# Output phase of an adaLN / S4 / SwiGLU kernel: the layout of the convolution's z rows for six token tiles, and the place of the block sums of x

## The chip, the cores and the metric

The kernel runs on one NeuronCore of a Trainium2 chip. The metric is the device time of one execution in microseconds (us). The engines are named as the profile names them: PE (matmul), PEld (weight load), DVE (vector), ACT (scalar), POOL and SP (which here only issues DMAs). ACT and POOL issue DMAs too; the profile calls the issuing side SPq, ACTq and POOLq.

## The reference

```python
x = A_u                                            # 1 x 2048 x 640, float32
mod = (_silu(c) @ w_mod).reshape(c.shape[0], 6, 1, -1)
sa, ca, ga, sb, cb, gb = (mod[:, 0], mod[:, 1], mod[:, 2], mod[:, 3], mod[:, 4], mod[:, 5])
h = _layernorm(x, axis=-1) * (1 + ca) + sa
x = x + ga * _A_ref(h, ...)                        # S4: K = sum_n C exp(dt A l) dt B, y = causal conv(h, K) + h * D
h = _layernorm(x, axis=-1) * (1 + cb) + sb
x = x + gb * _B_ref(h, w1, w3, w2)                 # (silu(h @ w1) * (h @ w3)) @ w2, inner width 1728
```

The long convolution is done through a two-stage transform by matmuls. The second stage of the inverse transform, per token tile, is what the change touches: y = i2 times z, added to x.

## The kernel before, in words

**Stages.** Up to about 366 us the kernel makes the S4 kernel K, transforms, multiplies and stores the half-inverted result `z` to DRAM (`zs`). Then come layernorm and the MLP on 16 token tiles of 128 tokens by 640 channels. The MLP works in two pairs of 1024 tokens: pair 0 is tiles 0 to 7, pair 1 tiles 8 to 15; within a pair, "A" is the first four tiles and "B" the last four. The inner width 1728 is cut into 14 blocks f of 128 (the last of 64).

**Products.** Operands are split into a high and a low part (`xA0` holds both, `gh` and `gl` a weight's), and each product takes three matmuls: high by high, high by low, low by high. In pair 0 the blocks f = 0, 13, 1, 2 (`simple`) are computed plainly (`plain`): first for A in this order, then for B in the order 2, 1, 13, 0. The other ten go through `seven`, which makes the four quarter products of a block out of seven by sums of x and of the weights. The sums of x are `x_sums` (DVE subtractions on the raw tiles s0 to s8) and `x_sum_split` (an ACT cast and a DVE subtraction for each of T10, T20, T40 and T11, T21, T41). The split of the B operands themselves is in `x_turn` and `x_split`: four transposes, ACT's affine step into a room s, ACT's cast to the high part, DVE's subtraction for the low part. The last of the five is T31 (k = 1). In `plain` the B operands are used in the order k = 4, 0, 2, 3, 1, that is xB4, T30, xB2, xB3, T31.

**Output phase.** `outputs` multiplies h with w2 in 28 steps (14 for A, 14 for B). A step has a w2 load issued on ACT's queue for four steps ahead (`load(n + 4, S)`), the operands of the next step (`operands(n + 1)`: ACT casts gh and uh, DVE makes gl and ul), the side work `side(n)`, and then 15 matmuls. Inside it `in_order[0]` is set, so each engine keeps the order of the program; the helper that records this is line 114, which is why the profile shows nearly every instruction at L114.

**Side work.** In pair 0's output phase `prepare` makes tiles 8 to 15 ready for pair 1. Per tile: `x_get` issues the loads on SP (x, and z from `zs`), `x_mid` multiplies z by `i2` into two PSUM banks, adds to x, and takes the layernorm's statistics, `x_norm` normalizes on ACT, and `turn_a` or `turn_b` transposes. The steps are fixed by tables:

```python
mids = (3, 4, 5, 6, 8, 9, 10, 12)
norms = (5, 6, 7, 8, 11, 12, 13, 15)
gets = (0, 0, 1, 2, 3, 4, 4, 6)
homes = (("xA0", "xA1"), ("xA2", "xA3"), ("xA4", "xB2"), ("xB3", "xB4"), ("T40", "T20"), ("T10", "T30"),
         None, None)
```

`homes` gives the first six of these tiles two rooms each to hold z, which are operand rooms of pair 0 that are no longer read; the last two use a `z_tile` of their own (name A).

**z in a tile.** A tile's z has 64 rows (two of them, real and imaginary, for each of 32), 4 token blocks b and 5 channel blocks k of 128. Channel blocks 0 and 1 go to partitions 0 to 63 and blocks 2, 3 and 4 to partitions 64 to 127, so that two row groups of PE work side by side. `z_load` issues one DMA per channel block. In `x_mid` each (token block, row group) pair is one matmul with 64 rows and 32 output columns: eight in all, on eight different parts of the array, 256 wide for the lower rows and 384 wide for the upper (`ZW`).

**DMA counters.** The framework gives each DMA of the hardware queues one of eight completion counters, DMAHW0 to DMAHW7, in turn as they stand in the program; SP and ACT share them. Before it is issued, a DMA waits until the last DMA on its counter has landed. In the built program T40's first transfer waits on DMAHW6, and the w2 loads for later steps on the counters of xA, xB and T transfers.

Of the kernel before, what the change touches and what calls it, by code (L numbers as in the profile page):

```python
# [9 lines left out]
F32 = mybir.dt.float32  # L10
# [12 lines left out]
DC = 128  # L23
NDC = D // DC
# [95 lines left out]
def tile_kernel(ctx: ExitStack, tc: tile.TileContext, a):  # L120
    nc = tc.nc
    V, S, G, PE = nc.vector, nc.scalar, nc.gpsimd, nc.tensor
# [8 lines left out]
    i2 = cp.tile([P, NA], F32, name="i2")  # L131
# [10 lines left out]
    V, S, G, PE, Q = (InOrder(tc, e, (front,)) for e in (nc.vector, nc.scalar, nc.gpsimd, nc.tensor, nc.sync))  # L142
# [633 lines left out]
    def zj(k, j):  # L776
        return zs[k, j % 4, j // 4].rearrange("l c f d -> (c f) l d")
# [66 lines left out]
        moments.extend((mv, rs))  # L844
        return power

    def z_load(z, j, ks, q=nc.sync, b0=0):

        nb = z.shape[1]
        for k in ks:  # L850
            hh = int(k > 1)
            kk = k - 2 * hh
            ins = q.dma_start(z[hh * 64:hh * 64 + 64, :, kk * DC:kk * DC + DC], zj(k, j)[:, b0:b0 + nb])
        return ins

    def x_tile():
# [5 lines left out]
    def z_tile():  # L862
        z = tz.tile([P, SD, 3, NA], F32, name="A")
        return z.rearrange("p k s b -> p (k s b)").rearrange("p (b d) -> p b d", b=4)

    ZW = (2 * DC, 3 * DC)
# [136 lines left out]
    for word in FRONT:  # L1003
        name, k = word[:2].rstrip("+"), int(word[len(word[:2].rstrip("+")):])
# [25 lines left out]
    for rnd in range(NS // EB):  # L1030
        if 2 <= rnd < 7:
            late_load(rnd - 2)
        for word in ROUND:
            name, k = word[:2].rstrip("+-"), EB * rnd + int(word[len(word[:2].rstrip("+-")):])
# [16 lines left out]
    for tk in range(NS + 1, LAG + 8 * NDC + 2):  # L1051
# [17 lines left out]
        i = tk - 1 - LAG - 8 * NDC + 8  # L1069
# [37 lines left out]
    V, S, G, PE = (InOrder(tc, e, (in_order,)) for e in (nc.vector, nc.scalar, nc.gpsimd, nc.tensor))  # L1107
    SQ = InOrder(tc, nc.sync, (in_order, sp_order))
# [3 lines left out]
    def bank(g):  # L1112
        return psG.tile([P, 512], F32, name="ps", tag="g") if g else psA.tile([P, 512], F32, name="ps", tag="acc")
# [13 lines left out]
    def pair_tile(name, dt=F32R):  # L1127

        return wq.tile([P, 2, 512], dt, name=name)
# [20 lines left out]
    def x_get(j, x, loaded=False, homes=None):  # L1150

        if homes:
            zs_ = [pair_tile(n, F32).rearrange("p a b -> p (a b)")[:, :768].rearrange("p (b d) -> p b d", b=2)
                   for n in homes]
        else:
            zs_ = [z_tile()]
        with tc.issue_after(zlast[0].ins):
            if not loaded:
                SQ.dma_start(x, a["x"][j * P:(j + 1) * P, :])
            for i, z in enumerate(zs_):  # L1160
                z_load(z, j, range(NDC), SQ, 2 * i)
        return [x, [zs_[b * len(zs_) // 4][:, b % (4 // len(zs_))] for b in range(4)]]

    def x_mid(j, got, g):

        x, z = got
        py = [bank(g) for _ in range(2)]
        for b in range(4):
            for hh in range(2):
                r, c = slice(hh * 64, hh * 64 + 64), slice(b * NA, b * NA + NA)  # L1170
                n = ZW[hh]
                PE.matmul(py[hh][c, :n], i2[r], z[b][r, :n], start=True, stop=True, tile_position=(r.start, c.start))
        for hh in range(2):
            h = slice(hh * 256, hh * 256 + ZW[hh])
            V.tensor_tensor(x[:, h], py[hh][:, :ZW[hh]], x[:, h], op=OP.add)
        got.extend(ln_stats(xp, x))
        G.dma_start(xs[j], x)
# [8 lines left out]
    ends = [None, None]  # L1186

    def x_split(name, xf):
        t = pair_tile(name)
        ends[0] = S.copy(t[:, 0], xf)  # L1190
        ends[1] = V.tensor_tensor(t[:, 1], xf, t[:, 0].bitcast(F32), op=OP.subtract)
        return t[:, 0], t[:, 1]
# [26 lines left out]
    def x_sums(i, which=range(4)):  # L1219

        if 0 in which:
            xraw["s", i] = xraw["A", i], xraw["A", i + 2], xraw["B", i], xraw["B", i + 2]
        b11, b21, b12, b22 = xraw["s", i]
        for n in which:
            to, l, r = ((b11, b12, b11), (b12, b22, b12), (b22, b22, b11), (b21, b21, b22))[n]
            V.tensor_tensor(to, l, r, op=OP.subtract)
        xraw["T1", i], xraw["T2", i], xraw["T4", i] = b11, b22, b21

    def x_sum_split(i, names=("T1", "T2", "T4")):
        for n in names:  # L1230
            xop[n, i] = x_split(f"{n}{i}", xraw[n, i])
# [44 lines left out]
    def plain_weights(f, after=None):  # L1276
        g = split(weight(f, "wg"), WS, ("gh", "gl"), after)
        return g, split(weight(f, "wu"), WS, ("uh", "ul"), after) if f < NFT - 1 else None
# [36 lines left out]
    def block_split(W):  # L1315
        W[2] = split(W[0], WS, ("gh", "gl"))
        W[3] = split(W[1], WS, ("uh", "ul"), part=slice(2, KD))
        return W
# [211 lines left out]
    for pair in range(2):  # L1530
        q0 = 2 * pair
        hA, hB = {}, {}
        simple = (0, last_f, 1, 2) if pair == 0 else (last_f,)
        rest = [f for f in range(last_f) if f not in simple]
        side = []
        ws = plain_weights(simple[0], last_sum if pair == 0 else None)
        W = None
        if pair:
            in_order[0] = True
            W = block_split(blocks(rest[0]))  # L1540
            w_sums(W, range(4))
            w_split(W, (1, 0, 2, 3))
            in_order[0] = False
        if pair == 0:
            tiles = []
            x_first(tiles)
            for k in range(KD):
                turn_a(0, tiles, k, 0)
            tiles = []
            sp_order[0] = True  # L1550
            got = [x_get(4, x5[0], True)]
            fetch(last_f, "wg")
            got.append(x_get(5, x5[1], True))
            fetch(1, "wg")
            fetch(1, "wu")
            got += [x_get(6, x_place("T40")), x_get(7, x_place("T20"))]
            sp_order[0] = False
            mid = lambda i: (x_mid(4 + i, got[i], 0), x_norm(4 + i, got[i], tiles))
            turn = lambda *ks: [turn_b(1, tiles, k, 0) for k in ks]
            side = [lambda: mid(0), lambda: (mid(1), mid(2)), lambda: mid(3), lambda: None,  # L1560
                    lambda: turn(4, 0, 2), lambda: turn(3, 1)]

        def beside(end):
            if side:
                with tc.issue_after(end.ins):
                    side.pop(0)()

        for n, f in enumerate(simple):
            hA[f] = h_tile()
            ws = ws or plain_weights(f, ends if pair == 0 and n == 1 else None)  # L1570
            end = plain("A", f, hA[f], ws, pair == 0, beside)
            if n < len(simple) - 1:
                ws = None
            beside(end)
            if pair == 0 and n == 1:
                with tc.issue_after(power.ins):
                    for j, (x, z, st) in enumerate(early):
                        G.dma_start(xs[j], x)

        for n, f in enumerate(simple[::-1]):  # L1580
            hB[f] = h_tile()
            ws = ws or plain_weights(f)
            plain("B", f, hB[f], ws)
            ws = None
            if pair == 0 and n < 2:
                x_sums(n)
                x_sum_split(n)
        for i in range(2):
            x_late(i)
        before = output  # L1590
        free = []
        order = rest[:10] + ([0, last_f, 1, 2] if pair == 0 else [last_f] + rest[10:])
        output = outputs(q0, order, (hA, hB), prepare(q0 + 2, 1, x4) if pair == 0 else lambda n: None, pair == 1)
        if W is None:
            W = block_split(blocks(rest[0]))
            w_sums(W, range(4))
            w_split(W, (1, 0, 2, 3))
        for n, f in enumerate(rest):
            nxt = block_split(blocks(rest[n + 1])) if n + 1 < len(rest) else None
            if n < 12:  # L1600
                free = free or places(3)
                hA[f] = free.pop(0)
            else:
                hA[f] = h_tile()
            hB[f] = h_tile()
            if nxt is None:
                next(output)
            seven(W, hA[f], hB[f], nxt)
            next(before, None)
            if pair == 0 and n == len(rest) - 4:  # L1610
                for i in range(4):
                    x4.append(x_tile())
                    nc.sync.dma_start(x4[i], a["x"][(8 + i) * P:(9 + i) * P, :])
            W = nxt
        next(output)
# [52 lines left out]
```

## Time and profile before

| what | value |
|---|---|
| time, median of 3 runs | 936.25 us (935.79 to 938.29) |
| the profiled execution | 939.53 us |
| its span | 937.6 us |
| granted PE clock over the span | 0.97 |
| output steps of pair 0, first products | 557.09 us |
| stretch of step 3's `x_mid` block to step 9's | 567.38 to 599.91 us |
| inner products of pair 0's B part, begin | 410.03 us |

A row of the page gives busy time and share of the span; a row of a window gives the stretch, its length and what each engine was busy in it. Idle time of an engine counts only where another waits for it: PE is the busiest engine, so the question for any stretch is what ends PE's waits in it. The names stand for the program's tiles with the numbers left out: `xA`, `xB` and `T` are rooms, `zs` the z in DRAM, `rw` a raw weight, `ps` a PSUM bank.

### The profile page before, as it was taken

To read this page: it belongs to the slowest core of one execution; us is meant where nothing else is said; L and a number is where in the kernel's file an instruction comes from. 1 tells how busy PE (TensorE), PEld (TensorE's weight loads), DVE (VectorE), ACT (ScalarE), POOL (GpSimd) and SP (SyncE) were. 2 spreads that over 40 slices of the span, in tenths; PEclk is the share of its full clock that TensorE was granted. 3 is DMA by queue.
4 is the path that set the end of the run, shared out by engine and by line. 5 is a ranking of instruction groups with operands and counts; after the bars stand their busy time and mean duration, and the time that the engine had idled before them with its cause. 6 is when DMAs were issued, how large, how long until landed. Compare 5 with 4: busy or idle time off the path is not lost.

```text
span 937.6 us, 20100 instructions
## 1 busy us (share of the span) xinstructions
PE 875.5 (93%) x8036; PEld 668.3 (71%) x8036; DVE 700.2 (75%) x1209; ACT 541.3 (58%) x747; POOL 272.7 (29%) x285
## 2 busy tenths in 40 slices
PE   4888879999998898999999999899999999999997
PEld 2545456666666576788888886578888888888786
DVE  5899889999999967685666665677976666654684
ACT  6988889999999542474333332475633333323332
POOL 3333434553454221223222202210332222200341
PEclk9977789999999998999999999999999999999999
DMA  9664375676566968942121227946311322123352
GB/s 270 217 222 175 133 211 179 212 192 192 171 210 191 299 202 227 290 149 75 56 57 57 57 82 213 260 148 195 101 57 56 113 57 57 56 87 97 98 187 93
DMA packets 103808, 140.68 MB, mean 150 GB/s; under 512 B 20420, under 2 KB 62916, under 8 KB 103716
## 3 DMA queue, kind: packets, MB, share of 16 engines
q1 hardware_dynamic: 93012, 113.71, 40.2%
q10 hardware_dynamic: 8272, 18.16, 6.4%
q0 software_dynamic: 2432, 7.54, 2.5%
q8 instruction: 63, 1.03, 0.5%
q14 instruction: 29, 0.24, 0.1%
HBM read 107.92 MB, written 31.46 MB: 149 GB/s over the span
## 4 chain that ended last, share of the span: by engine, by line
PE 74%; ACT 9%; DVE 8%; issue 3%; SPq 3%; DMA 3%; DVEq 0%; ACTq 0%
PE ps L114 54%; PE p L114 7%; PE pz L114 4%; PE pt L114 3%; SPq L114 3%; PE pk L114 2%; PE pa L114 2%; ACT A L114 2%; ACT cs L114 1%; DVE uk L114 1%; DVE u L114 1%; ACT ph L114 1%; PE pu L114 1%; ACT uk L114 1%; ACT L114 1%
## 5 line engine op out<-in xcount | busy, mean ns | idle before, releaser
L114 DVE TENSOR_TENSOR s<-ps,s 128x512 f32<-128x512 f32 x138 | 94.9, 687 | 82.5 <-PE ps L114 82.2
L114 ACT CAST gh<-rw 128x640 fp32r<-128x640 f32 x87 | 63.3, 728 | 128.3 <-PE ps L114 86.4
L114 DVE TENSOR_TENSOR gl<-rw,gh 128x640 fp32r<-128x640 f32 x87 | 78.0, 896 | 69.0 <-ACT gh L114 68.6
L114 POOL TENSOR_TENSOR S<-rw 128x256 f32<-128x256 f32 x46 | 36.9, 805 | 234.9 <-DVE S0l L114 157.4
L114 PE MATMUL ps<-gh,uh 128*128 128x512 f32 x224 | 88.1, 393 | 0.0
L114 PE MATMUL ps<-gl,uh 128*128 128x512 f32 x224 | 87.7, 392 | 0.0
L114 PE MATMUL ps<-xA,gh 128*128 128x512 f32 x280 | 87.6, 391 | 0.0
L114 PE MATMUL p<-uk,s 128*64 128x256 f32 x576 | 71.6, 391 | 15.2 <-DVE Y L114 3.9
L114 POOL TENSOR_TENSOR ph<-thi,iota 128x1376 int32<-128x1376 int32 x20 | 51.2, 2562 | 117.8 <-DVE A L114 103.6
L114 DVE TENSOR_TENSOR E<-A,cs 128x1024 f32<-128x1024 f32 (+1 forms) x80 | 80.6, 1019 | 1.9 <-PE pk L114 1.3
L114 PE MATMUL ps<-gh,ul 128*128 128x512 f32 x208 | 81.6, 392 | 0.0
L114 ACT ACTIVATE A<-pa 128x1024 f32<-128x1024 f32 (+1 forms) x80 | 64.4, 815 | 10.2 <-PE pa L114 9.8
L114 PEld LDWEIGHTS p<-uk,s 128*64 128x64 f32 x576 | 41.3, 138 | 36.9 <-DVE Y L114 5.6
L114 PEld LDWEIGHTS ps<-xA,gh 128*128 128x128 f32 x280 | 52.3, 188 | 12.5 <-ACT xA L114 0.7
L114 DVE TENSOR_TENSOR A<-A,ph 128x1024 f32<-128x1024 f32 x40 | 54.1, 1357 | 0.8
L114 PE MATMUL ps<-xA,gl 128*128 128x512 f32 x140 | 54.5, 389 | 0.0
L114 PE MATMUL pt<-s,K 128*64 128x128 f32 x640 | 45.1, 284 | 6.1 <-ACT uk L114 5.9
L114 PEld LDWEIGHTS ps<-gl,uh 128*128 128x128 f32 x224 | 42.5, 190 | 9.1
L114 PEld LDWEIGHTS ps<-gh,uh 128*128 128x128 f32 x224 | 42.5, 190 | 9.0 <-DVE h L114 0.2
L114 ACT ACTIVATE s<-ps 128x512 f32<-128x512 f32 (+1 forms) x33 | 19.7, 597 | 45.8 <-PE ps L114 45.8
L114 POOL TENSOR_TENSOR rw<-rw,gbr 128x512 f32<-128x512 f32 x14 | 20.4, 1458 | 88.7 <-DMA rw<-in_w_dram 77.3
L114 PEld LDWEIGHTS pt<-s,K 128*64 128x64 f32 x640 | 35.6, 140 | 14.5 <-ACT uk L114 9.7
(224 smaller groups left out, 2227.2 us busy)
## 6 DMA issues: line engine op xcount, KB each, us to landing
rw<-in_w_dram ACTq DMA_DIRECT2D x44, 320.0 KB, 3.0
us<-u SPq DMA_DIRECT2D x16, 640.0 KB, 3.5
rw<-in_wg_dram SPq DMA_DIRECT2D x31, 320.0 KB, 3.0
s<-in_s_dram SPq DMA_DIRECT2D x36, 256.0 KB, 4.0
i<-in_i_dram SPq DMA_DIRECT2D x36, 256.0 KB, 4.7
rw<-in_wu_dram SPq DMA_DIRECT2D x28, 320.0 KB, 2.9
uk<-us SPq DMA_DIRECT2D x16, 512.0 KB, 5.6
zs<-zt SPq DMA_DIRECT2D x16, 512.0 KB, 4.7
```

The costliest lines, as they stand in the source:

```text
L114: ins = fn(*args, **kw)
```

## The change

Four edits, all in the file's output-phase code:

1. `x_get`, for the six tiles with two rooms: z is laid by channel block. The first ("wide") room holds blocks 0 and 1 in the lower partitions and 2 and 3 in the upper ones, the second ("narrow") room block 4. Five transfers of 64 x 4 x 128 instead of ten of 64 x 2 x 128.
2. `x_mid` goes over the parts: for these tiles the upper rows' 384-wide matmul becomes one of 256 and one of 128, 12 matmuls instead of 8. The two tiles in a `z_tile` keep 8.
3. `x_sums` and `x_sum_split` of pair 0 are issued after `turned`, the last operand split.
4. `z_load` loses the argument that chose token blocks.

```diff
     def x_get(j, x, loaded=False, homes=None):

         if homes:
-            zs_ = [pair_tile(n, F32).rearrange("p a b -> p (a b)")[:, :768].rearrange("p (b d) -> p b d", b=2)
-                   for n in homes]
+            wide, narrow = (pair_tile(n, F32).rearrange("p a b -> p (a b)") for n in homes)
+            wide = wide.rearrange("p (k b d) -> p k b d", k=2, b=4)
+            z = [wide[:, 0], wide[:, 1], narrow[:, :4 * DC].rearrange("p (b d) -> p b d", b=4)]
+            use = [(0, 2 * DC, wide.rearrange("p k b d -> p b k d")), (2 * DC, 3 * DC, z[2])]
         else:
-            zs_ = [z_tile()]
+            t = z_tile()
+            z = [t[:, :, k * DC:k * DC + DC] for k in range(3)]
+            use = [(0, 3 * DC, t)]
         with tc.issue_after(zlast[0].ins):
             if not loaded:
                 SQ.dma_start(x, a["x"][j * P:(j + 1) * P, :])
-            for i, z in enumerate(zs_):
-                z_load(z, j, range(NDC), SQ, 2 * i)
-        return [x, [zs_[b * len(zs_) // 4][:, b % (4 // len(zs_))] for b in range(4)]]
+            for k in range(NDC):
+                hh = int(k > 1)
+                r = slice(hh * 64, hh * 64 + 64)
+                SQ.dma_start(z[k - 2 * hh][r], zj(k, j))
+        return [x, use]

     def x_mid(j, got, g):
...
                 r, c = slice(hh * 64, hh * 64 + 64), slice(b * NA, b * NA + NA)
-                n = ZW[hh]
-                PE.matmul(py[hh][c, :n], i2[r], z[b][r, :n], start=True, stop=True, tile_position=(r.start, c.start))
+                for lo, hi, part in z:
+                    n = min(hi, ZW[hh]) - lo
+                    if n > 0:
+                        rhs = part[r, b] if len(part.shape) == 4 else part[r, b, :n]
+                        PE.matmul(py[hh][c, lo:lo + n], i2[r], rhs, start=True, stop=True,
+                                  tile_position=(r.start, c.start))
...
+        turned = ends[1]
         for n, f in enumerate(simple[::-1]):
...
             if pair == 0 and n < 2:
-                x_sums(n)
-                x_sum_split(n)
+                with tc.issue_after(turned.ins):
+                    x_sums(n)
+                    x_sum_split(n)
```

SP, before: the z loads of tiles 8 to 13 in their rooms, from the start of the output phase, up to the one in T40 and T20, with its x load (`xm`) ahead of it.

```order
230 L114 DMA xA0_6646<-zs_58 64x2x128 x5
231 L114 DMA xA1_6647<-zs_58 64x2x128 x5
232 L114 DMA xA2_6658<-zs_58 64x2x128 x5
233 L114 DMA xA3_6659<-zs_58 64x2x128 x5
234 L114 DMA xA4_6695<-zs_58 64x2x128 x5
235 L114 DMA xB2_6696<-zs_58 64x2x128 x5
236 L114 DMA xB3_6732<-zs_58 64x2x128 x5
237 L114 DMA xB4_6733<-zs_58 64x2x128 x5
238 L114 DMA xm_6769<-in_x_dram 128x640
239 L114 DMA T40_6770<-zs_58 64x2x128 x5
240 L114 DMA T20_6771<-zs_58 64x2x128 x5
```

SP, after the change, the same tiles:

```order
230 L114 DMA xA0_6646<-zs_58 64x4x128 x4
231 L114 DMA xA1_6647<-zs_58 64x4x128
232 L114 DMA xA2_6653<-zs_58 64x4x128 x4
233 L114 DMA xA3_6654<-zs_58 64x4x128
234 L114 DMA xA4_6685<-zs_58 64x4x128 x4
235 L114 DMA xB2_6686<-zs_58 64x4x128
236 L114 DMA xB3_6717<-zs_58 64x4x128 x4
237 L114 DMA xB4_6718<-zs_58 64x4x128
238 L114 DMA xm_6749<-in_x_dram 128x640
239 L114 DMA T40_6750<-zs_58 64x4x128 x4
240 L114 DMA T20_6751<-zs_58 64x4x128
```

Each pair of rooms now gets four and one transfers instead of five and five, and the x load stands behind half as many. The tiles in a `z_tile` keep their five.

PE, before: the `x_mid` block of the sixth tile (rooms T10 and T30); behind the operation stand the PSUM bank and the two operands, then rows x columns of the output.

```order
1425 L114 MATMUL ps_7087<-T10_6832,i2_64 32x256
1426 L114 MATMUL ps_7088<-T10_6832,i2_64 32x384
1427 L114 MATMUL ps_7087<-T10_6832,i2_64 32x256
1428 L114 MATMUL ps_7088<-T10_6832,i2_64 32x384
1429 L114 MATMUL ps_7087<-T30_6833,i2_64 32x256
1430 L114 MATMUL ps_7088<-T30_6833,i2_64 32x384
1431 L114 MATMUL ps_7087<-T30_6833,i2_64 32x256
1432 L114 MATMUL ps_7088<-T30_6833,i2_64 32x384
```

PE, after, the first half of the same block:

```order
1446 L114 MATMUL ps_7077<-T10_6811,i2_64 32x256
1447 L114 MATMUL ps_7078<-T10_6811,i2_64 32x256
1448 L114 MATMUL ps_7078<-T30_6812,i2_64 32x128
1449 L114 MATMUL ps_7077<-T10_6811,i2_64 32x256
1450 L114 MATMUL ps_7078<-T10_6811,i2_64 32x256
1451 L114 MATMUL ps_7078<-T30_6812,i2_64 32x128
```

Every token block now reads both rooms, and the 128-wide matmul follows directly on the 256-wide one of the same row group and column group; before, each matmul of the block was on a part of the array of its own.

DVE, before: the last operand splits of B in pair 0 (a room's name on both sides) with the sums of x (s on both sides) and their splits (T10, T20, T40, T11), up to the weights of the block f = 13 (gl_5407).

```order
545 L114 TENSOR_TENSOR s4_5239<-s6_5249,s4_5239 128x512
546 L114 TENSOR_TENSOR xB2_5251<-s6_5249,xB2_5251 128x512
547 L114 TENSOR_TENSOR h_5195<-ps_5254,s8_5270 128x512
548 L114 TENSOR_TENSOR s6_5249<-s6_5249,s0_4908 128x512
549 L114 TENSOR_TENSOR T10_5333<-s0_4908,T10_5333 128x512
550 L114 TENSOR_TENSOR s2_4928<-s2_4928,s6_5249 128x512
551 L114 TENSOR_TENSOR xB3_5280<-s7_5278,xB3_5280 128x512
552 L114 TENSOR_TENSOR T31_5290<-s5_5288,T31_5290 128x512
553 L114 TENSOR_TENSOR T20_5336<-s6_5249,T20_5336 128x512
554 L114 TENSOR_TENSOR T40_5339<-s2_4928,T40_5339 128x512
555 L114 TENSOR_TENSOR s1_4918<-s5_5288,s1_4918 128x512
556 L114 TENSOR_TENSOR gl_5407<-rw_5404,gh_5406 128x640
```

DVE, after, from xB2's split on:

```order
544 L114 TENSOR_TENSOR xB2_5251<-s6_5249,xB2_5251 128x512
545 L114 TENSOR_TENSOR h_5195<-ps_5254,s8_5270 128x512
546 L114 TENSOR_TENSOR xB3_5280<-s7_5278,xB3_5280 128x512
547 L114 TENSOR_TENSOR T31_5290<-s5_5288,T31_5290 128x512
548 L114 TENSOR_TENSOR s0_4908<-s4_5239,s0_4908 128x512
549 L114 TENSOR_TENSOR s1_4918<-s5_5288,s1_4918 128x512
550 L114 TENSOR_TENSOR s4_5239<-s6_5249,s4_5239 128x512
551 L114 TENSOR_TENSOR T10_5333<-s0_4908,T10_5333 128x512
552 L114 TENSOR_TENSOR s6_5249<-s6_5249,s0_4908 128x512
553 L114 TENSOR_TENSOR s5_5288<-s7_5278,s5_5288 128x512
554 L114 TENSOR_TENSOR s2_4928<-s2_4928,s6_5249 128x512
555 L114 TENSOR_TENSOR h_5293<-ps_5310,s8_5326 128x512
```

The last three splits follow each other with only h_5195 between, and the sums stand behind T31. Seven rows on are the same weights:

```order
555 L114 TENSOR_TENSOR h_5293<-ps_5310,s8_5326 128x512
556 L114 TENSOR_TENSOR T20_5336<-s6_5249,T20_5336 128x512
557 L114 TENSOR_TENSOR T40_5339<-s2_4928,T40_5339 128x512
558 L114 TENSOR_TENSOR s7_5278<-s7_5278,s1_4918 128x512
559 L114 TENSOR_TENSOR T11_5394<-s1_4918,T11_5394 128x512
560 L114 TENSOR_TENSOR s3_4938<-s3_4938,s7_5278 128x512
561 L114 TENSOR_TENSOR T21_5397<-s7_5278,T21_5397 128x512
562 L114 TENSOR_TENSOR gl_5407<-rw_5404,gh_5406 128x640
```

All sums and their splits stand behind T31, and gl_5407 is seven places behind h_5293, where it was three places ahead of it. On ACT the cast for T10 leaves the place ahead of xB3's affine step in the same way.

More of the change, by code (lines that the diff above doesn't have):

```diff
@@ L845, in x_stats, with z_load @@
         return power
-    def z_load(z, j, ks, q=nc.sync, b0=0):
-        nb = z.shape[1]
+    def z_load(z, j, ks, q=nc.sync):
         for k in ks:
@@ L852, in z_load @@
             kk = k - 2 * hh
-            ins = q.dma_start(z[hh * 64:hh * 64 + 64, :, kk * DC:kk * DC + DC], zj(k, j)[:, b0:b0 + nb])
+            ins = q.dma_start(z[hh * 64:hh * 64 + 64, :, kk * DC:kk * DC + DC], zj(k, j))
         return ins
```

## The prediction

> **What bounds the kernel now.** I read the page first, then the windows of the output phase, then the chain of waits through it.
>
> ```profile
> PE 875.5 (93%) x8036; PEld 668.3 (71%) x8036; DVE 700.2 (75%) x1209; ACT 541.3 (58%) x747; POOL 272.7 (29%) x285
> PE 74%; ACT 9%; DVE 8%; issue 3%; SPq 3%; DMA 3%; DVEq 0%; ACTq 0%
> 573.00:596.00 23.00, 20.31 (x122) 12.96 (x113) 12.33 (x26) 7.47 (x11) 7.48 (x20) 0.98 0.88 234
> 622.00:937.60 315.60, 310.05 (x1382) 255.55 (x1380) 210.07 (x332) 125.94 (x223) 65.02 (x66) 1.00 0.31 97
> ```
>
> PE is the bound over the span (93%), and it is almost full from 622 us to the end (310.05 of 315.60). So a microsecond that PE gets back before 622 us moves the end by about a microsecond. The first two rows are the page's busy times and the chain by engine; the others give a stretch, its length, then busy time of PE, PEld, DVE, ACT, POOL, the granted clock, the DMA share and GB/s. Between 573 and 596 us PE loses 2.7 us while the DMA engines are at 0.88. The chain, which follows PE almost everywhere, leaves it there:
>
> ```profile
> 573.67 4.67 DMA T<-zs
> ...
> 582.30 3.80 DMA T<-zs
> ...
> 586.17 0.33 ACTq L114
> ...
> 586.61 0.73 ACT gh L114
> ...
> 588.84 4.05 PE ps L114 x26
> ```
>
> The columns are start, length and what. A transfer of z into room T has to land; then ACT issues a w2 load, then casts gh, and only after DVE's part does PE go on. The w2 load does not read z. It waits because each hardware transfer gets one of eight completion counters, shared by the SP and ACT queues, and cannot be issued before the last transfer on its counter has landed. Late z transfers on SP thus hold ACT, whose casts stand behind the load:
>
> ```profile
> ACT gh L114 <- DMA T<-zs: 9.4, 2, 5.1
> DVE gl L114 <- ACT gh L114: 21.0, 12, 3.7
> 545.72 17.14 SPq L114 DMA_DIRECT2D xA<-zs  x25
> 581.68 6.45 SPq L114 DMA_DIRECT2D T<-zs  x10
> 588.82 3.75 SPq L114 DMA_DIRECT2D A<-zs  x5
> ```
>
> The first two rows are waits (total, times, longest), the others SP's timeline. SP issues 64 KB transfers at 17.14/25 = 0.69 us each, and the 128 KB ones of room A at 3.75/5 = 0.75. SP is limited by the number of transfers, hardly by their size.
>
> What PE loses is read stretch by stretch, cut at the starts of the inverse-transform blocks of `x_mid` and of the 15 w2 products of a step:
>
> ```profile
> 567.38:568.18 0.80, 0.80 (x17) 0.18 (x16) 0.04 (x1) 0.00 (x0) 0.00 (x0) 1.00 0.76 215
> 568.18:571.82 3.64, 3.64 (x19) 2.74 (x15) 1.24 (x2) 1.25 (x2) 0.00 (x0) 1.00 0.73 189
> 571.82:573.43 1.61, 1.61 (x18) 0.54 (x17) 1.57 (x5) 0.00 (x0) 0.00 (x0) 1.00 0.53 153
> 581.50:583.01 1.51, 1.51 (x17) 0.52 (x16) 1.48 (x5) 0.00 (x0) 0.00 (x0) 1.00 0.85 278
> 583.01:587.90 4.89, 3.74 (x17) 2.74 (x15) 1.06 (x3) 1.29 (x3) 1.71 (x5) 1.00 0.74 216
> 587.90:592.01 4.11, 4.00 (x15) 2.73 (x16) 2.78 (x7) 0.78 (x1) 0.88 (x3) 1.00 0.87 239
> 592.01:594.21 2.20, 0.88 (x18) 0.18 (x17) 0.54 (x1) 1.30 (x3) 0.83 (x3) 1.00 1.21 196
> 594.21:599.91 5.70, 5.59 (x15) 3.90 (x16) 3.40 (x7) 2.84 (x4) 0.00 (x0) 0.70 1.10 277
> 595.20:598.60 3.40, 3.40 (x8) 2.72 (x9) 1.23 (x2) 1.99 (x3) 0.00 (x0) 0.50 1.10 327
> ```
>
> An `x_mid` block that waits for nothing takes 0.80, a step's products 3.64 (the first two rows). The excess is 0.81 and 0.71 in two blocks (busy on paper, but waiting for DVE to empty the PSUM of the block before, which stood behind gl), 1.25 and 0.47 in the next products, 1.40 and 2.06 in the last two rows of the sequence: **6.70 us**. Of this 1.70 is the half clock of the last row (3.40 us at 0.50).
>
> **The change, part by part.**
>
> ```profile
> 556.86 0.39 PE L114 MATMUL ps<-xA,ul 128*128 128x512 f32 x1
> ```
>
> *Transfers.* The row is the last product that reads room xA4. Six tiles take five transfers instead of ten: 30 issues fewer, some 30 x 0.69 = 21 us of SP time between 545 and 588 us. The last z of room T was issued at 581.68 + 6.45 = 588.1 us. In the new order ten transfers stand ahead of room xA4, which PE reads until its output products begin at about 557 us; the 20 from there on at 0.75 end at 572, with two x loads between them at about 575. The last of the six tiles is multiplied in step 9, some 20 us later, and every w2 load should find its counter landed. SP's next stop is the x load behind room T, which needs the norm of step 5; what it brings is multiplied from step 10 on. So I count the stalls as gone. What is late next is PE itself: gh of a step needs only the end of the products two steps earlier, a whole step (4.4 us) ahead, and in the step from 587.90 to 594.21 DVE was busy for 2.78 + 0.54 = 3.3 us and ACT for 2.1. The clock part is less sure. Two PE gaps of about one size preceded (4.89 - 3.74 = 1.15 us idle, then 2.20 - 0.88 = 1.32) and only the second was followed by half clock, so I count half of it: 6.70 - 0.85 = **-5.85**, with ends at -5.0 and -6.7.
>
> The Trainium skill (TensorE: Matmul & The Clock Gate, Part 1: The HAM clock gate) says that the gate judges a free-running window of about 3.4 us. The stretch of 3.40 us above agrees in length; by that rule the same gap may or may not be punished in another execution, and this term would be -5.0 or -6.7.
>
> *Matmuls.* The six blocks take 12 matmuls instead of 8. The 384-wide one of rows 64 to 127 becomes 256 plus 128 on the same part of the array.
>
> ```profile
> 577.05 0.53 PE L114 MATMUL ps<-xA,i 64*32 64x256 f32 x4
> 577.29 0.39 PE L114 MATMUL ps<-xA,i 64*32 64x256 f32 x2
> 577.40 0.50 PE L114 MATMUL ps<-xA,i 64*32 64x384 f32 x2
> ```
>
> Each matmul makes two passes (16 records for 8 matmuls), and the eight run side by side: the second 256-wide passes start 0.24 us after the first ones, the 384-wide 0.35 after. So 128 columns are worth 0.11 and a 128-wide pass about 0.13. The longest part was 2 x 0.35 = 0.70 and becomes 2 x 0.24 + 2 x 0.13 = 0.74: some 0.05 a tile, **+0.3** for six. The low end is 0. The high end is that the 128-wide matmul, which must wait for its own part of the array, holds back the columns behind it; it is the rival below. The row for that is the adaLN product at 17.7 us, four 256-wide matmuls on the column groups 0 to 3, then two of 128 on groups 0 and 1, then the next four:
>
> ```profile
> L114 PE MATMUL pm<-uk,sc x6: 421/634/634, 17.3 to 17.7; 128*32 128x256 f32 x4, 128*32 128x128 f32 x2
> L114 PE MATMUL pm<-uk,sc x8: 421/634/634, 17.3 to 17.7; 128*32 128x256 f32 x6, 128*32 128x128 f32 x2
> ```
>
> These are what was running in the stretches 17.70 to 17.73 and 17.73 to 17.76. Two new 256-wide ones began while the 128-wide passes had just begun on groups 0 and 1, so they belong to groups 2 and 3, ahead of those for 0 and 1 that stand before them in the program. Blocked columns did not hold the others; I take +0.3.
>
> The Trainium skill (TensorE: Matmul & The Clock Gate, Part 3: Packing small matmuls) says instead that matmuls start and end strictly in program order. By that rule the rival's price holds; this trace does not agree with it.
>
> *Sums of x.* They now stand behind the last operand split, T31.
>
> ```profile
> 412.45 0.62 PE L114 MATMUL ps<-xB,uh 128*128 128x512 f32 x2
> 413.47 0.50 PE L114 MATMUL ps<-xB,gh 128*128 128x512 f32 x1 [0.40 <-DVE xB L114]
> 424.93 0.39 PE L114 MATMUL ps<-xB,gl 128*128 128x512 f32 x1
> 412.12 0.69 DVE L114 TENSOR_TENSOR s<-s,s 128x512 f32<-128x512 f32 x1
> 412.73 0.69 DVE L114 TENSOR_TENSOR xB<-s,xB 128x512 fp32r<-128x512 f32 x1
> 417.87 0.69 DVE L114 TENSOR_TENSOR h<-ps,s 128x512 f32<-128x512 f32 x1
> ```
>
> Two products of 0.23 from 412.45 on would have let the next begin at 412.90; it began at 413.47, after xB3's split. Three operations of 0.6 stand in front of that split on DVE and go behind it; what is left is ACT's cast, so it should be ready some 0.6 us sooner: **-0.57**, or 0 at worst. The price could come back later: gl_5407, the weights of the plain product at 424.5 us, stands seven places behind the h that was at 417.87 in the new order. With that h at 417.3 it would begin at 417.3 + 7 x 0.6 = 421.5 and be done at 422.3, and its first use (424.93 before) moves to 424.4: 2 us to spare. The block sums' own readers come at 435 us. Cost 0.
>
> *Sum:* -5.85 + 0.3 - 0.57 = **-6.1 us** for the profiled execution: its own time is 939.53 us (span 937.6), so 933.4. The median of the runs is 936.25, 3.3 lower; the losses are waits in the program's order, so I carry the difference over: **930.1**.
>
> **The rivals.**
>
> *Half comes back.* The same bytes now come faster, and w2 loads compete: SP would ask for 128 KB per 0.75 us (175 GB/s) and ACT for 320 KB per 4.4 (74): 249 together. For it: room T's transfers already waited with the share at 0.88 for 234 GB/s. Against it: 327 were moved in the stretch of half clock. If two steps still waited, half of 5.85 would stay: 933.1.
>
> *Nothing comes back.* Another transfer on a shared counter, or the DVE, takes the place of T<-zs, as each step has a w2 load that must get a counter. Only the sums would gain: 936.0.
>
> *Blocked columns, slower.* If passes start strictly in program order in `x_mid`, each column group waits for the two passes of the 128-wide matmul before it: 3 x (0.48 + 0.13) + 0.48 + 0.27 = 2.6 us a block instead of 0.7: +1.9 x 6 = 11.4, less 6.4 from the rest: 941.2. It decides from about +1.1 a block, at which all gains are used up. For it: there are two row groups here, which the adaLN product lacks. Against it: the two rows above.
>
> *Late sums.* If DVE is over 2 us later than I laid out, PE waits at 424 us, one for one; 1 to 2 us, so 931 to 932, and more would need ACT to be late as well.
>
> **How the numbers follow.** Forecast 0.62; half comes back 0.18; nothing 0.09; blocked columns 0.08; late sums with more than their gain 0.03. The forecast's own range runs from all terms at their good ends (-6.7 - 0.57 = -7.3, 929.0, less 0.8 for the runs' scatter) to 932. Taking in the half case with the scatter of the runs shown (up to 2.0 above the median) gives 928.2 to 935.5; outside are blocked columns, nothing and some of the last. About 0.3% (2.8 us, 933.4) is what a measurement of this kernel can tell from no change. Faster by more: the forecast, two thirds of the half case and most of the late sums, 0.76; within: nothing and the rest of the half case, 0.15; slower by more: 0.09.
>
> **What would show it.** SP's z timeline of room T should end near 575 us, not 588; no wait of ACT gh for a zs transfer should be left; the windows between `x_mid` starts should read 4.4 to 4.6 us, and the ninth step's block should start near 594 instead of 599.9; the blocks themselves near 0.85 us; PE's wait for DVE xB at 413 us should be gone, and none should appear at 424. I am wrong if blocks last over 1.5 us, or if ACT still waits for a transfer before gh at steps 6 to 8.

## The result, and the profile after

The changed kernel takes **930.63 us** (median of 6 runs, 928.19 to 934.73) where the kernel before, on the same chip, takes 937.75 (median of 6, 935.79 to 939.5). The ratio is 0.9934, with a 95% interval of 0.9916 to 0.9953. Forecast were 930.1 us and a change of -6.1; measured by the medians is a change of -7.1, and by the ratio -6.2 (-4.4 to -7.9). Two later sets of the same kernel gave ratios of 0.9951 and 0.9938 (below), that is -4.6 and -5.8 us.

The profiled execution after is one of 928.99 us, its span 927.0. The page's busy times and its chain by engine:

```profile
PE 868.3 (94%) x8084; PEld 666.4 (72%) x8084; DVE 699.7 (75%) x1209; ACT 541.5 (58%) x747; POOL 274.1 (30%) x285
PE 76%; DVE 11%; ACT 8%; issue 3%; DMA 2%; SPq 0%; DVEq 0%; ACTq 0%
```

SPq has gone from 3% of the chain to 0. The windows of the output phase after, cut like those of before at the starts of the `x_mid` blocks and of the products (length first, then busy time of each engine, granted clock, DMA share, GB/s):

```profile
563.60:564.43 0.83, 0.83 (x25) 0.53 (x25) 0.00 (x0) 0.72 (x2) 0.00 (x0) 1.00 1.08 230
564.43:568.05 3.62, 3.62 (x19) 2.74 (x15) 3.32 (x7) 0.52 (x1) 0.12 (x1) 1.00 1.12 245
568.05:568.88 0.83, 0.83 (x25) 0.54 (x24) 0.00 (x0) 0.72 (x2) 0.67 (x3) 1.00 1.19 209
576.96:577.79 0.83, 0.83 (x25) 0.53 (x25) 0.00 (x0) 0.72 (x2) 0.73 (x2) 1.00 1.10 241
581.32:584.81 3.49, 3.49 (x16) 2.63 (x14) 1.43 (x2) 2.08 (x3) 1.71 (x5) 1.00 1.16 260
584.81:585.64 0.83, 0.83 (x25) 0.54 (x24) 0.00 (x0) 0.06 (x1) 0.00 (x0) 1.00 1.03 384
585.64:589.27 3.63, 3.63 (x20) 2.74 (x16) 2.90 (x6) 2.02 (x3) 0.00 (x0) 1.00 1.10 310
```

PE is busy for the whole of each of these stretches, these blocks take 0.83 us, and the clock is 1.00. The block of step 9 starts at 589.27, not 599.91 (3.1 of these 10.6 us are the scatter of the first piece in the table below). The waits in the output phase, first one of PE and one of ACT before, then those after and SP's timeline:

```profile
PE ps L114 <- ACT uh L114: 2.5, 2, 1.3
ACT gh L114 <- PE ps L114: 11.0, 6, 4.2
```

```profile
PE ps L114 <- ACT idle L114: 0.2, 1, 0.2
```

```profile
ACT gh L114 <- PE ps L114: 28.2, 14, 3.2
ACT gh L114 <- DMA xm<-in_x_dram: 3.4, 1, 3.4
```

```profile
561.06 4.73 SPq L114 DMA_DIRECT2D T<-zs  x5
...
568.82 3.75 SPq L114 DMA_DIRECT2D T<-zs  x5
```

ACT's casts now wait mostly for PE, which is how it should be: they are ahead of it. In this profile no wait for a zs transfer is left, and room T is out at 572.6 us, not 588.1 (some 576 when the start of step 3's block is laid on that of before). Two other profiles of the same kernel, y0 and z4, do have such waits, of 3.7 and 3.8 us; here is y0's:

```profile
ACT gh L114 <- DMA T<-zs: 3.7, 1, 3.7
```

PE does not feel them (stretches of 25.70 and 25.67 us in the table further down). So the change does not free ACT of every wait on a counter; it makes the waits short enough for the step by which the casts are ahead.

Two executions differ by some us before they reach any wait that the edits move, so the profiles are compared in four pieces, with starts from PE's timelines: up to the first product with xB (f = 2 of B), from there to the block of step 3, from there to the block of step 9, and the rest.

| piece | before | after | difference |
|---|---|---|---|
| to the first product with xB | 410.03 | 406.89 | -3.14 |
| to step 3's block (the sums) | 157.35 | 156.71 | -0.64 |
| to step 9's block (the transfers) | 32.53 | 25.67 | -6.86 |
| to the end of the span | 337.7 | 337.7 | 0.0 |

The first piece is taken as scatter: it holds at most a few of the moved sums, PE waits for none of them there, and three profiles of the changed kernel alone (406.89, 407.49 and 410.56 us) differ by more than its 3.14 us. The last piece shows no loss of what was gained ahead of it, but its agreement here is luck: in y0 and z4 it is 337.0 and 338.5.

### The profile page after: what moved, and what is told of

Its sections match the earlier page's. It is cut to its first block, busy times and chain, and to the rows that moved or that the text cites. A ratio compares the mean times of both kernels' runs of the same rounds, so it can differ in the third digit from the quotient of the medians.

```text
span 927.0 us, 20146 instructions
## 1 busy us (share of the span) xinstructions
PE 868.3 (94%) x8084; PEld 666.4 (72%) x8084; DVE 699.7 (75%) x1209; ACT 541.5 (58%) x747; POOL 274.1 (30%) x285
## 4 chain that ended last, share of the span: by engine, by line
PE 76%; DVE 11%; ACT 8%; issue 3%; DMA 2%; SPq 0%; DVEq 0%; ACTq 0%
PE ps L114 58%; PE p L114 6%; PE pz L114 3%; PE pt L114 2%; PE pk L114 2%; DVE A L114 2%; DVE E L114 2%; ACT cs L114 2%; PE pa L114 1%; DVE uk L114 1%; ACT A L114 1%; DVE u L114 1%; ACT uk L114 1%; DMA s<-in_s_dram 1%; ACT L114 1%
```

## The experiments

**Theory A**: SP's number of issues made it fall behind PE; each w2 load on ACT waits for a transfer eight places ahead of it in the program; so ACT, and PE behind it, were held to SP's pace. **Rivals**: the sums carry a good part; the longer pieces per row carry it; the late z itself holds PE. In the table, "sums" is the second piece of the table above and "stretch" the third; "to step 11" goes on from the same start to the first transposes of step 11 (PE's `ps<-ident,T` there), for some kernels lose time right behind the stretch. Ratios are to the kernel before, run beside each.

| run | transfers a tile | sums, us | stretch, us | to step 11, us | ratio (95%) |
|---|---|---|---|---|---|
| before | 10 | 157.35 | 32.53 | 42.12 | |
| changed | 5 | 156.71 | 25.67 | 35.28 | 0.9934 (0.9916 to 0.9953) |
| x1_transfers_alone | 5 | 157.35 | 25.67 | 35.29 | 0.9957 (0.9940 to 0.9975) |
| x2_sums_alone | 10 | 156.75 | 31.21 | 42.16 | 0.9989 (0.9976 to 1.0002) |
| x3_ten_transfers | 10, new layout | 156.75 | 33.47 | 43.61 | 1.0011 (0.9995 to 1.0027) |
| x4_w2_on_pool | 10, w2 on POOL | 157.40 | 25.63 | 36.54 | 0.9954 (0.9937 to 0.9971) |
| y0_changed_again | 5 | 156.75 | 25.70 | 35.31 | 0.9951 (0.9933 to 0.9969) |
| y1_changed_w2_on_pool | 5, w2 on POOL | 156.74 | 25.67 | 35.29 | 0.9954 (0.9936 to 0.9972) |
| y2_ten_in_T_rooms | 5 for four, 10 for two | 156.75 | 27.54 | 37.15 | 0.9955 (0.9941 to 0.9968) |
| y3_ten_in_x_rooms | 10 for four, 5 for two | 156.71 | 31.70 | 41.32 | 1.0009 (0.9994 to 1.0024) |
| z1_six_per_tile | 6 | 156.71 | 25.66 | 35.28 | 0.9896 (0.9876 to 0.9917) |
| z2_eight_per_tile | 8 | 156.71 | 25.67 | 35.43 | 0.9932 (0.9908 to 0.9955) |
| z3_six_again | 6 | 156.70 | 26.24 | 36.45 | 0.9926 (0.9906 to 0.9946) |
| z4_changed_beside_six | 5 | 156.71 | 25.67 | 35.29 | 0.9938 (0.9916 to 0.9959) |

**x1: the transfers and the matmuls alone.**

```diff
-                with tc.issue_after(turned.ins):
-                    x_sums(n)
-                    x_sum_split(n)
+                x_sums(n)
+                x_sum_split(n)
```

> Theory A (fewer issues on SP, so the shared counters come free, so ACT's w2 loads and casts are no longer held): from the block of step 3 to the block of step 9 PE takes 25.5 to 26.5 us as in the changed kernel (25.67; before 32.53), no wait of ACT gh for a zs transfer; PE's wait of 0.4 us for DVE xB at the f = 2 product of B is back; ratio 0.993 to 0.996. Rival (a good part of the gain is the place of the sums): ratio 0.997 or above although the stretch is short.

The stretch is the changed kernel's to the hundredth, and PE's wait at the sums is back (one short wait of ACT gh for a zs transfer, A<-zs, 1.2 us, was not expected):

```profile
PE ps L114 <- DVE xB L114: 0.4, 1, 0.4
```

**x2: the sums alone** (the last hunk of the change on the kernel before).

> Theory A: PE's wait for DVE xB is gone, worth 0.4 to 0.6 us (ratio 0.999 to 1.000); the stretch from step 3's block to step 9's stays at 31 to 33.5 us and ACT gh still waits for T<-zs. Rival (the sums carry the gain): ratio 0.997 or less.

Together these two say which edit does what: the sums are worth 0.60 to 0.64 us in the traces, and without the new transfers ACT still waits (first its waits, then two windows):

```profile
ACT gh L114 <- DMA T<-zs: 10.5, 2, 5.8
ACT gh L114 <- DMA xB<-zs: 3.8, 1, 3.8
```

```profile
577.00:580.40 3.40, 1.98 (x9) 0.98 (x7) 1.54 (x3) 2.07 (x3) 0.31 (x1) 1.00 0.62 192
583.80:587.20 3.40, 2.48 (x11) 1.39 (x9) 1.50 (x3) 2.07 (x3) 0.61 (x2) 1.00 0.77 216
```

PE loses 1.42 and 0.92 us in the two windows of this kernel, and the clock stayed at 1.00. The stretch is 1.3 us shorter than before's, but that is not a gain: the next block, of step 9, takes 2.17 us instead of 0.81, and up to step 11 this kernel takes 42.16 us where before took 42.12, with half clock.

**x3: the new layout with ten transfers.**

```diff
-                SQ.dma_start(z[k - 2 * hh][r], zj(k, j))
+                if homes:
+                    for b in (0, 2):
+                        SQ.dma_start(z[k - 2 * hh][r, b:b + 2], zj(k, j)[:, b:b + 2])
+                else:
+                    SQ.dma_start(z[k - 2 * hh][r], zj(k, j))
```

> The changed kernel with each of the five transfers cut into two of 64x2x128 again: same rooms, same 12 matmuls, same place of the sums, 30 issues more. Theory A: the stretch is back at 31 to 33.5 us, ACT gh waits for zs transfers again, ratio 0.999 to 1.001. Rival (the layout in the room, pieces of 2 KB instead of 1 KB, makes the transfers fast): the stretch stays below 28 us, ratio 0.993 to 0.996.

Same rooms, same matmuls, same bytes: the gain is gone. Not the layout, the count. The stretch of 33.47 holds some 3.4 us at half clock again (580.2 to 583.6; the window shown takes in a little more):

```profile
580.40:583.80 3.40, 3.40 (x14) 2.51 (x9) 0.67 (x4) 0.77 (x2) 1.70 (x5) 0.53 0.76 137
```

**x4: the link from SP to ACT cut, on the kernel before.** All 60 z transfers stay on SP; only the w2 loads leave the shared counters and ACT's line.

```diff
-            load(n + 4, S)
+            load(n + 4, S if last else G)
```

> The kernel before with the w2 loads of pair 0's output phase issued on POOL's queue, whose counters are its own; all 60 z transfers stay on SP. Theory A: ACT gh waits for no zs transfer, the stretch is 26 to 29 us (a wait for the z of the last room T may be left, as its transfers are out only near 588 us), ratio 0.994 to 0.998. Rival (the late z itself holds PE, or SP's number of issues as such): the stretch stays at 31 us or more, ratio 0.999 or above.

The stretch shows the whole gain: 25.63 us, better than the 26 to 29 expected. The waits of ACT, SP's timeline, and PE behind the stretch:

```profile
ACT gh L114 <- PE ps L114: 32.5, 16, 3.2
```

```profile
577.95 6.45 SPq L114 DMA_DIRECT2D T<-zs  x10
```

```profile
595.61 0.87 PE L114 MATMUL ps<-A,i 64*32 64x384 f32 x14 [0.71 <-DMA A<-zs]
```

SP was still issuing room T until 584.4 us, 20.6 us behind the start of step 3's block where it was 20.7 before, and PE did not mind. So the late z of the six rooms did not hold PE: it was the w2 loads behind shared counters, with ACT's casts behind them. This is the run that settles the mechanism, though it cuts two things at once: the loads leave both the shared counters and ACT's queue, and neither was cut alone. A one-line edit reaches the stretch that the change reaches. It does not reach all of the gain: with SP still late, the z of the next tile (name A) holds PE in step 10, and up to step 11 this kernel takes 36.54 us, 1.26 more than the changed one.

**y0 and y1: the changed kernel again, and with the link cut too.**

> The changed kernel again, on the chip and beside the runs of the kernel before that the next three share. Theory A: ratio 0.992 to 0.996, the stretch from step 3's block to step 9's at 25.6 to 25.9 us.

> The changed kernel with the w2 loads of pair 0's output phase on POOL's queue. Theory A (PE is already full there, so the last coupling between SP and ACT costs nothing): same as the changed kernel, ratio of the two 0.998 to 1.002, stretch 25.6 to 25.9 us, and ACT gh waits for no SP transfer. Rival (a wait on a shared counter still costs PE in many executions that the one trace does not show): 0.2 to 0.4% below the changed kernel.

Both edits together bring no more than the change (0.9954 against 0.9951, stretch 25.67 against 25.70): PE is full in this phase, so the 3.4 to 4.8 us that ACT still waits at a time for a transfer in the changed kernel cost nothing.

**y2 and y3: which tiles matter.** As x3, with the cut only for the last two of the six tiles, or only for the first four.

> The changed kernel with ten transfers again for the last two of the six tiles (rooms T), five for the first four: 10 issues more than the changed kernel. Theory A: room T is out by about 577 us instead of 588, the stretch is 25.6 to 28 us, ratio to before 0.993 to 0.997. Rival (room T's transfers themselves, the ones in the waits' rows, are what counts): stretch 29 us or more, ratio 0.997 or above.

> The changed kernel with ten transfers again for the first four tiles (rooms xA and xB), five for the last two: 20 issues more than the changed kernel. Theory A: SP is as late as before at the first T (about 573 us by before's time), so the waits at steps 4 and 6 (0.8 and 0.7 us) stay and those of steps 7 and 8 shrink: stretch 27 to 30 us, ratio 0.996 to 0.999. Rival (room T's transfers are what counts): stretch below 26.5 us, ratio 0.993 to 0.995.

y2's stretch and ratio came out as expected, though room T was out only at 582.3 us, not 577. One wait is back, at step 8, where the cast stood behind two w2 loads:

```profile
585.03 3.21 ACTq L114 DMA_DIRECT2D rw<-in_w_dram  x2
588.28 0.72 ACT L114 CAST gh<-rw 128x640 fp32r<-128x640 f32 x1 [6.58 <-DMA xm<-in_x_dram]
```

y3 was a miss on the bad side: 31.70 us and a ratio of 1.0009, where 27 to 30 and 0.996 to 0.999 were expected. PE's blocks, ACT's casts and a window of it:

```profile
568.82 1.60 PE L114 MATMUL ps<-xA,i 64*32 64x256 f32 x24
590.53 0.50 PE L114 MATMUL ps<-uh,gh 128*128 128x512 f32 x1 [2.12 <-ACT uh L114]
```

```profile
572.09 0.73 ACT L114 CAST gh<-rw 128x640 fp32r<-128x640 f32 x1 [4.14 <-DMA xB<-zs]
589.23 0.72 ACT L114 CAST gh<-rw 128x640 fp32r<-128x640 f32 x1 [6.05 <-DMA A<-zs]
```

```profile
590.53:593.93 3.40, 3.37 (x8) 2.35 (x9) 0.88 (x2) 1.33 (x2) 0.00 (x0) 0.59 1.09 277
```

I had taken the backlog to be undone once the last two tiles were short. It is not: the waits go on through the A tile. As I read it, the early w2 loads are late, so the casts, the norms and the x loads behind them are late. The window also holds most of 3.4 us at half clock (591.2 to 594.6), worth about 1.7 us. The rooms named in the waits of before were T; the tiles that made them late were the four ahead of it. The two runs differ in the number of issues as well, 10 against 20 more than the changed kernel, but z2 below has 18 more, spread over all six tiles, and loses nothing in its stretch; so the total alone does not set the loss.

**z1 and z2: how many are too many.** As x3, with only block 4 cut in two (six a tile), or blocks 0, 2 and 4 (eight).

> The changed kernel with six transfers a tile (block 4 cut in two) for the six tiles. Theory B, as the runs so far left it: what counts is whether SP's issues for a tile fit into one PE step (4.45 us with a block, 3.4 without), since each w2 load waits for the transfer eight places ahead of it; 6 x 0.69 = 4.1 us fits: stretch 25.6 to 26.2 us, ratio 0.993 to 0.997. Rival (each issue more costs its share, 30 issues for about 6 us): stretch 26.7 to 27.3 us.

> The changed kernel with eight transfers a tile (blocks 0, 2 and 4 cut in two). Theory B: 8 x 0.69 = 5.5 us does not fit into a step of 4.45, SP falls back by about 1 us a tile where ten fall back by 2.5: part of the waits returns at the last steps, stretch 26.5 to 29 us, ratio 0.995 to 0.999. Rival (share per issue): stretch 28.5 to 30 us; rival (only ten is too many): 25.6 to 26.2 us.

Both keep the full stretch. Eight was expected to lose some and did not: theory B's rule, that a tile's issues must fit into a step, is too strict, and a cost per issue is ruled out. ACT waits for room T in the second kernel and PE does not feel it:

```profile
ACT gh L114 <- DMA T<-zs: 7.3, 2, 4.1
```

Casts are made one step ahead of their use, and that step absorbs it. The limit lies between eight and ten a tile; where, and whether it is by pace or by which transfer stands eight places ahead, was not tried.

**z3 and z4: six against five.** z1's ratio of 0.9896 stood below the changed kernel's with the same stretch in the trace, so both ran side by side.

> The kernel of z1 (six transfers a tile) again, beside the changed kernel on one chip. Its four runs stood 0.4 to 0.5% below the ratios of the changed kernel, with the same stretch in the trace. Theory: that was scatter between chips and executions; ratio to before 0.993 to 0.997 and within 0.2% of the changed kernel's in the same call; stretch 25.6 to 25.8 us. Rival: six is better than five, ratio 0.990 to 0.992.

> The changed kernel on the same chip. Ratio to before 0.993 to 0.997, stretch 25.6 to 25.8 us.

0.9926 and 0.9938, with intervals that overlap almost wholly: no difference between six and five is shown. z3's profile lost 0.6 us in step 8, which puts its stretch of 26.24 outside the 25.6 to 25.8 expected, and as much again in step 9's block (36.45 us up to step 11). Side by side, no version beat the changed kernel.

## Why the prediction was right, point by point

- **What bounds.** Right: what PE got back before 600 us arrived at the end, as far as the traces can tell (the last piece is 337.7 in both, and 337.0 to 338.5 among the profiles of the changed kernel).
- **Luck in the total.** Forecast was 930.1 and 930.6 was measured, but the kernel before was at 937.75 in the same set, 1.5 us above the median that the forecast started from; by change, -6.1 stands against -7.1 by the medians and -6.2, -4.6 and -5.8 by the three ratios.
- **Transfers**, forecast -5.85 with ends at -5.0 and -6.7: the trace shows -6.86 in the stretch, with about 0.2 the other way for the larger blocks in it. Shown by x1 (edit alone), x3 (count put back) and x4 (link cut). In repeated executions the edit alone gave 0.9957, some 4.0 us (2.3 to 5.6): the low end of the forecast lies inside that, -5.85 just outside, and why the traces show more than the times is not known. Together with x2's 0.9989 that is 0.9946, inside the interval of the changed kernel.
- **Half of the clock term.** The profiles agree that a gap may or may not be followed by half clock: before, x3 and y3 have such a window behind gaps of 1.3, 2.3 and 2.1 us, x2 and y2, with gaps of 1.7 and 1.3 us, have none. This is in keeping with the free-running window that the Trainium skill describes (TensorE: Matmul & The Clock Gate, Part 1: The HAM clock gate); its windows are about 3.4 us, the slow stretches here 3.4. How often it strikes was not measured. The term itself, 1.70 us that would be lost or not, is not borne out: x2, with the same transfers as before and no half clock, takes as long up to step 11 (42.16 against 42.12), for it waits longer elsewhere.
- **Matmuls**, forecast +0.3: 0.83 a block where 0.80 was, +0.03 x 6 = 0.2. The passes of the third block after:

```profile
572.51 0.68 PE L114 MATMUL ps<-xA,i 64*32 64x256 f32 x16
572.97 0.44 PE L114 MATMUL ps<-xB,i 64*32 64x128 f32 x8
```

  All sixteen 256-wide passes, of all four column groups, begin ahead of the first 128-wide one, though in the program the first 128-wide matmul stands ahead of six of the 256-wide. Blocked columns did not hold the rest, with two row groups either, and the rival at 941 is out. The rule of strict program order (TensorE: Matmul & The Clock Gate, Part 3: Packing small matmuls, in the Trainium skill) does not hold for starts here.
- **Sums**, forecast -0.57: -0.64 in the pair of profiles, -0.60 in x2. PE's products run on without a gap, and gl_5407 has its margin:

```profile
409.29 0.39 PE L114 MATMUL ps<-xB,uh 128*128 128x512 f32 x1
409.51 0.46 PE L114 MATMUL ps<-xB,gh 128*128 128x512 f32 x1
421.16 0.39 PE L114 MATMUL ps<-xB,gl 128*128 128x512 f32 x1
```

```profile
418.39 0.82 DVE L114 TENSOR_TENSOR gl<-rw,gh 128x640 fp32r<-128x640 f32 x1
```

  gl is ready at 419.2 and used at 421.16: 2 us to spare, as worked out.
- **Half comes back**, the rival on contention: its cause was real and its price was not. Everything in flight took longer (first before, then after):

```profile
rw<-in_w_dram ACTq DMA_DIRECT2D x9, 320.0 KB, 3.0
T<-zs SPq DMA_DIRECT2D x20, 64.0 KB, 4.1
```

```profile
rw<-in_w_dram ACTq DMA_DIRECT2D x11, 320.0 KB, 7.1
T<-zs SPq DMA_DIRECT2D x10, 128.0 KB, 6.5
```

  The last number is the median of us from issue to landing. A load is issued some 15 us ahead of its cast (561.92 and 577.07 us for one of them after), so 7 us still fit.
- **Where the reasoning was loose.** "SP is limited by the number of transfers" was right, but the prediction let a reader think that z for room T was what PE missed. x4 shows that this z can be as late as before without holding PE. "Every w2 load should find its counter landed" was wrong: in the profile after, two w2 loads are held from 578.92 on until an x load has landed, and ACT waits 3.4 us before the cast in step 7; y0 and z4 wait for T<-zs. By its letter this is one of the signs of being wrong that the prediction named, and it cost PE nothing. The gain came because the waits became short, not because they ended. The range's upper end, too, does not follow from its terms: 933.1 and 2.0 make 935.1, not 935.5.

## What to carry to other kernels

When an engine's compute stands behind a DMA issue that waits for an unrelated transfer, look at what links the two queues (here completion counters taken in turn): either the link can be cut, by putting the loads on a queue with counters of its own, or the slower queue can be given fewer, larger transfers until it keeps ahead. Here the fewer transfers alone brought as much as both together; the cut link alone left a late transfer, for which PE then waited. The wait's row names the transfer that is late, not the ones that made it late: count back over the queue's whole backlog before choosing which to merge.

## What the runs showed of the hardware that was not expected

- A w2 load on a busy core took 7.1 us to land where it had taken 3.0, with the DMA share above 1.0 in each of the windows quoted from 563 to 589 us, though the same bytes were moved.
- The kernels took between 405.65 and 411.17 us to reach the first product with xB, ahead of every wait that the edits move, and the changed kernel alone between 406.89 and 410.56; the middle pieces repeat to some hundredths where nothing waits (156.70 to 156.75, and 25.63 to 25.70). For an edit of less than 0.3%, such pieces of a profile are a sharper measure than the times, as long as the last piece is not among them (337.0 to 338.5 for the changed kernel) and the cut lies behind the last wait.
- In the two sets of z1 and z3 one and the same kernel gave 0.9896 and 0.9926, with intervals that barely overlap (up to 0.9917, and from 0.9906): an interval from four runs says less than it seems.
